# Linear attention into a top-2 mixture of experts: token weights gathered with the row of x, a PSUM bank of its own for the last list products, ScalarE without the list loads

## The chip, the core and the metric

The kernel runs on one core of one Trainium2 chip. Its engines work in parallel, each through its own queue in order: TensorE (PE: matmuls, with weight loads PEld beside them), VectorE (DVE), ScalarE (ACT), GpSimd (POOL, which also issues the indirect DMAs) and SyncE (SP, which issues the plain DMAs). They meet at semaphores, so an instruction that waits holds up all behind it in its own queue. The metric is the device time of one launch in microseconds (us); lower is better.

## The reference, cut to what matters

Block-wise causal linear attention with a decay per head, then a noisy top-2 mixture of experts over its 3072 output rows.

```
x = attention(q, k, v, lam)          # B=4, H=8, S=768, D=64 -> x: 3072 x 512
noisy = x @ w_gate + log1p(exp(x @ w_noise)) * noise        # 3072 x 8
top2 = the two largest of noisy, weights = softmax of the two
for e in range(8):                   # w1[e]: 512 x 1024, w2[e]: 1024 x 512
    rows = tokens with e among their two
    out[rows] += weight * (relu(x[rows] @ w1[e]) @ w2[e])
```

All of it is float32. The kernel makes each expert product of three matmuls, high part by high part, high by low and low by high.

## The kernel before

**Attention.** `for t in range(NST)` runs 12 steps of two 128-token chunks each. A step's output `xo` is multiplied by the gate's weights (`products`, `logits`) and transposed to rows of tokens by `store_x` (TensorE's transposes L419, ScalarE's copy into `xc` L421, SyncE's store into `x_tok` in DRAM L423). ScalarE also takes the attention's transposes out of PSUM (L305 `kT`, L319 `qT`). The loads of weights and their split into a high part (ScalarE L753) and a low part (VectorE L754) are spread over the steps by the tables `LOADS` and `SPLITS`.

**Routing.** The 24 chunks go in three groups (`GB` = 0, 8, 16, 24). For each, `gate` finds the two experts of a token on VectorE, `weights` their two weights on GpSimd (into `wd`, 128 x chunks x 8), `count` and `route` each token's place in its experts' lists. A Python generator per group hands out its VectorE and GpSimd work in small pieces: `advance(n)` puts about n us of pieces behind what stands in the program at that point, so the order is fixed when the program is built, and each engine keeps to it.

**Lists.** The lists of tokens by expert are made by one-hot matmuls. For each unit of one or two chunks, `keys` writes two one-hot tables on VectorE (L578), `loads` makes two products of the second of them, one on ScalarE (L587, by the token's row `rowf`), one on VectorE (L590, by the chunk's number), and `enlist` multiplies the tables on TensorE (L599) into one bank of PSUM, `pL`. That bank also holds the gate's logits and the counts (L522). VectorE adds the result to `found`; `decode` turns it into integers `recs`, two for each place: the token, and where the weight lies in a table `wtab` in DRAM (four VectorE operations, the last of them L617).

**Experts.** `gather_rows` fetches a tile's 128 rows of x by an indirect DMA on GpSimd (L777), `gather_w` a tile's weights from `wtab` by another (L784). `trans_rows` transposes a tile (TensorE L793) and splits it into `xth` (ScalarE L795) and `xtl` (VectorE L796). `gemm1` (L809, with the evictions L815 on ScalarE and L819 on VectorE) and `gemm2` (L847) follow; experts 1 to 7 add what they make to the rows of `out` (gather L831, VectorE L859, scatter L866). The output is zeroed first by 24 plain DMAs (L879).

**The handover.** Expert 0 is started while the second and third group are still being routed, in parts of 2, 2 and 3 tiles (`PARTS0`): the first needs the lists of the first group, the second those of the second, the third those of the third. So the program after the attention runs: first two tiles transposed, first `gemm1`, between them the list products of the second group (`pv` as tables), second part with the gate of the third group in between, then `lists_done` in the middle of the `gemm2` of tile 2 (after 12 of its 24 matmuls, `MID`): the third group's list products, `recs`, then the gathers of the last three tiles of expert 0, of four tiles of expert 1, and of three tiles' weights. From there experts 1 to 7 run one after the other. A last loop (`For_i`) over overflowing tiles runs no times with this data.

Of the kernel before, what the change touches and what calls it, by code (L numbers as in the profile page):

```python
# [24 lines left out]
I32 = mybir.dt.int32  # L25
# [28 lines left out]
RW = 2  # L54
NTL = E * NT
NV = 2
HOT = 2 * (128 + NTL + NV * NTL)
# [8 lines left out]
SPLITS = {2: (1, 0), 3: (1, 1), 6: (1, 2), 7: (1, 3), 9: (2, 0), 10: (2, 1), 11: (2, 2)}  # L66
MID = 12
# [55 lines left out]
def kernel(  # L123
# [16 lines left out]
    x_tok = dram.tile([NTOK, DM], FT, name="x_tok")  # L140
    wtab = dram.tile([128 * NCH * E, 1], FT, name="wtab")
# [24 lines left out]
    zero = consts.tile([128, DM], FT, name="zero")  # L166
# [54 lines left out]
    for nm in ("kt", "qt", "vt"):  # L221
# [25 lines left out]
    WBASE = (BIG // TS) * E + TS * NCH * E  # L247
    wcol = consts.tile([128, E, NT], FT, name="wcol")
    nc.gpsimd.iota(wcol, pattern=[[1, E], [0, NT]], base=WBASE, channel_multiplier=0,
                   allow_small_or_imprecise_dtypes=True)  # L250
    destf = consts.tile([128, 2, NCH], FT, name="destf")
    recs = consts.tile([128, NTL, RW], I32, name="recs")
# [161 lines left out]
    def store_x(u):  # L414

        for a in range(2):
# [6 lines left out]
            nc.sync.dma_start(x_tok[g * C:(g + 1) * C, :], xc.rearrange("p d i -> p (d i)"))  # L423
# [66 lines left out]
    def weights(b):  # L490
# [92 lines left out]
    def loads(b, c, n, buf):  # L583
# [3 lines left out]
        nc.scalar.activation(mv[:, :, 1, :], hi, AF.Copy, scale=rowf)  # L587
# [6 lines left out]
    def enlist(some, start=True, stop=True):  # L594

        LP = pl[:, :NV * NTL]
        pairs = [(lo[:, k, :], mv[:, k, :]) for b, c, n, buf in some for lo, _, mv in (hot(buf, n),) for k in range(2 * n)]
        for k, (lo, mv) in enumerate(pairs):
            nc.tensor.matmul(LP, lo, mv, start=start and not k, stop=stop and k == len(pairs) - 1)  # L599
        b, c, n, _ = some[-1]  # L600
        RT[b]["listed"] = c + n
        if stop:
            LP = LP.rearrange("p (w j) -> p w j", w=NV)
            if "found" in RT:
                nc.vector.tensor_add(found, found, LP)
            else:
                nc.vector.tensor_copy(found, LP)
            RT["found"] = True

    def decode(s, out, n, base):  # L610

        v = nc.vector
        idf = rp.tile([128, 2, n], FT, name=f"idf{n > 1}")
        v.scalar_tensor_tensor(idf[:, 0], s[:, 0], float(TS), s[:, 1], op0=MULT, op1=ADD)
# [595 lines left out]
```

## Time and profile before

| what | us |
|---|---|
| median of 3 runs (lowest, highest) | 783.83 (781.5, 785.53) |
| the profiled execution | 789.62 |
| its span, first to last instruction | 787.7 |
| TensorE busy in the span | 740.5 (94%) |
| VectorE, ScalarE, GpSimd busy | 348.5, 227.8, 289.4 |

All views are of the one profiled execution; times in them are us from the start of its span. A view in order of time gives an instruction's start, its duration, and in brackets how long its engine had been idle before it and what ended that wait. "issue" means that the engine waited for nothing that the profile shows. Line numbers are those of the kernel before. [...]

### The profile page before, as it was taken

How to read it: one execution, taken by the hardware profiler on the slowest of the kernel's cores; microseconds unless marked ns; L12 is line 12 of the kernel's file. 1: busy time of each engine (PE TensorE's matmuls, PEld its weight loads, DVE VectorE, ACT ScalarE, POOL GpSimd, SP SyncE). 2: the span in 40 equal slices, each digit the busy share in tenths (PEclk: the TensorE clock that was granted, in tenths of full speed). 3: DMA queues.
4: the chain of work that ended last, by engine and by line, in shares of the span. 5: the costliest groups of instructions: out<-in, count | busy, mean ns of one | idle time of the engine just before them, and what ended most of it. 6: DMA issues, size and time to landing. Idle time of an engine off the chain costs nothing.

```text
span 787.7 us, 15593 instructions
## 1 busy us (share of the span) xinstructions
PE 740.5 (94%) x6170; PEld 627.1 (80%) x6170; DVE 348.5 (44%) x823; ACT 227.8 (29%) x395; POOL 289.4 (37%) x438
## 2 busy tenths in 40 slices
PE   6999988869979999999999999999999999999993
PEld 4888867768868888798878877987888898889882
DVE  5555777747414554452335232614343352335210
ACT  0355553541204332142214221413132142214100
POOL 2321333305070475325432743274324425222411
PEclk8899998978989999999999999999999999999997
DMA  7999983254080654444344333424442543321110
GB/s 171 198 270 256 238 217 116 103 208 167 4 248 27 175 154 136 156 121 119 92 151 130 101 108 137 138 75 139 126 134 56 173 157 103 91 95 36 50 53 22
DMA packets 90861, 103.45 MB, mean 131 GB/s; under 512 B 37222, under 2 KB 63462, under 8 KB 90784
## 3 DMA queue, kind: packets, MB, share of 16 engines
q1 hardware_dynamic: 77424, 66.11, 31.3%
q0 software_dynamic: 13360, 36.30, 13.9%
q8 instruction: 50, 0.82, 0.4%
q14 instruction: 27, 0.22, 0.1%
HBM read 77.75 MB, written 25.84 MB: 132 GB/s over the span
## 4 chain that ended last, share of the span: by engine, by line
PE 81%; issue 6%; DVE 3%; ACT 3%; DMA 2%; another core or an unknown queue 2%; POOL 1%; SPq 1%; ACTq 0%; POOLq 0%; DVEq 0%
PE pS L809 33%; PE pKV L847 15%; PE pO L847 14%; PE pS L793 3%; PE pS L344 3%; PE pO L356 2%; PE pKV L356 2%; PE pS L303 2%; PE pS L419 1%; PE pO L852 1%; PE pS L391 1%; PE pS L316 1%; DMA QS<-powd 1%; PE pKV L852 1%
## 5 line engine op out<-in xcount | busy, mean ns | idle before, releaser
L809 PE MATMUL pS<-xth,w1h 128*128 128x512 f32 (+3 forms) x544 | 184.8, 340 | 6.0 <-ACT xth L795 4.1
L809 PE MATMUL pS<-xtl,w1h 128*128 128x512 f32 (+3 forms) x544 | 183.2, 337 | 1.0 <-DVE xtl L796 0.7
L809 PE MATMUL pS<-xth,w1l 128*128 128x512 f32 (+3 forms) x544 | 183.0, 336 | 0.4 <-issue 0.4
L819 DVE SCALAR_TENSOR_TENSOR ht<-pS,ht 128x256 fp32r<-128x256 f32 (+3 forms) x176 | 76.3, 456 | 153.9 <-ACT ht L815 139.3
L847 PE MATMUL pO<-w2h,ht 128*128 128x512 f32 x384 | 126.9, 401 | 0.5 <-ACT ht L815 0.5
L847 PE MATMUL pKV<-w2h,ht 128*128 128x512 f32 x384 | 126.2, 400 | 0.0
L866 POOL DMA_INDIRECT out_dram<-ot,rec x46 | 60.4, 1313 | 172.0 <-DVE ot L859 160.8
L815 ACT ACTIVATE ht<-pS 128x512 fp32r<-128x512 f32 (+3 forms) x136 | 65.1, 483 | 189.5 <-PE pS L809 136.7
L809 PEld LDWEIGHTS pS<-xth,w1h 128*128 128x128 f32 x544 | 105.2, 193 | 16.3 <-ACT xth L795 4.8
L809 PEld LDWEIGHTS pS<-xtl,w1h 128*128 128x128 f32 x544 | 105.1, 193 | 10.0 <-DVE xtl L796 1.2
L809 PEld LDWEIGHTS pS<-xth,w1l 128*128 128x128 f32 x544 | 104.9, 193 | 9.9 <-issue 1.1
L795 ACT ACTIVATE xth<-pS 128x512 fp32r<-128x512 f32 (+2 forms) x53 | 30.0, 572 | 206.9 <-PE pS L793 205.3
L847 PEld LDWEIGHTS pO<-w2h,ht 128*128 128x128 f32 x384 | 72.3, 188 | 18.0 <-ACT ht L815 1.0
L847 PEld LDWEIGHTS pKV<-w2h,ht 128*128 128x128 f32 x384 | 72.3, 188 | 16.8
L847 PE MATMUL pKV<-w2l,ht 128*128 128x512 f32 x192 | 76.1, 396 | 0.0
L847 PE MATMUL pO<-w2l,ht 128*128 128x512 f32 x192 | 76.1, 396 | 0.0
L777 POOL DMA_INDIRECT xg<-x_tok,rec x46 | 48.9, 1062 | 14.3 <-issue 12.4
L831 POOL DMA_INDIRECT pv<-out_dram,rec x46 | 47.1, 1023 | 16.9 <-issue 13.6
L784 POOL DMA_INDIRECT wr<-wtab,rec x46 | 45.9, 997 | 16.0 <-issue 15.1
L859 DVE SCALAR_TENSOR_TENSOR ot<-pKV,wr,pv 128x512 f32<-128x512 f32 x21 | 15.8, 751 | 79.9 <-PE pKV L847 79.9
L859 DVE SCALAR_TENSOR_TENSOR ot<-pO,wr,pv 128x512 f32<-128x512 f32 x21 | 15.8, 751 | 79.7 <-PE pO L847 79.7
L332 POOL TENSOR_TENSOR kd<-kt,Mk 128x512 f32<-128x512 f32 x24 | 24.8, 1057 | 64.2 <-PE pR L391 27.5
(220 smaller groups left out, 1011.5 us busy)
## 6 DMA issues: line engine op xcount, KB each, us to landing
wst<-in_moe_w_dram SPq DMA_DIRECT2D x48, 512.0 KB
wst<-in_moe_w_dram SPq DMA_DIRECT2D x32, 256.0 KB
kt<-in_k_dram SPq DMA_DIRECT2D x12, 512.0 KB
qt<-in_q_dram SPq DMA_DIRECT2D x24, 256.0 KB
vt<-in_v_dram SPq DMA_DIRECT2D x12, 512.0 KB
x_tok<-xc SPq DMA_DIRECT2D x24, 256.0 KB
out_dram<-zero SPq DMA_DIRECT2D x24, 256.0 KB
xg<-x_tok,rec POOLq DMA_INDIRECT x46
```

Source lines behind the costliest of these rows:

```text
L332: nc.gpsimd.tensor_mul(kd[:, :, s], kt[:, :, s], mask(s, slice(0, HP), slice(C - 1, C)).to_broadcast([128, HP, 2, D]))
L356: nc.tensor.matmul(PO[u][a][half(g), hp, :], lhs, rhs, start=n == 1, stop=n == (12 if u % NW or a else 8))
L777: nc.gpsimd.indirect_dma_start(out=XG[t][:size(e, t)], out_offset=None, in_=x_tok[:rows, :], in_offset=bass.IndirectOffsetOnAxis(ap=REC[e, ...
L784: nc.gpsimd.indirect_dma_start(out=WR[e % 3][:n, t:t + 1], out_offset=None, in_=wtab, in_offset=bass.IndirectOffsetOnAxis(ap=REC[e, t][:, ...
L795: nc.scalar.activation(hi, p, AF.Copy)
L809: nc.tensor.matmul(p, W1[a][d][:, fs], xt(b, cs)[:, d], start=(d == 0 and i == 0), stop=(d == DB - 1 and i == 2))
L815: nc.scalar.activation(ht(e, 0, f, cs), p, AF.Relu)
L819: nc.vector.scalar_tensor_tensor(ht(e, 1, f, c), p[:, r], 0.0, ht(e, 0, f, c).bitcast(FT), op0=OP.max, op1=SUB)
L831: nc.gpsimd.indirect_dma_start(out=PV[t][:size(e, t), :], out_offset=None, in_=out, in_offset=bass.IndirectOffsetOnAxis(ap=REC[e, t][:, 0: ...
L847: nc.tensor.matmul(p, ht(e, a, f, cs), W2[b][f // 2][:, f % 2, :], start=(i == 0), stop=(i == len(terms) - 1))
L859: nc.vector.scalar_tensor_tensor(o, p, w, pv, op0=MULT, op1=ADD)
L866: st = nc.gpsimd.indirect_dma_start(out=out, out_offset=bass.IndirectOffsetOnAxis(ap=REC[e, t][:, 0:1], axis=0), in_=o, in_offset=None, bo ...
```

## The change

It has four parts.

1. The rows of `x_tok` grow from 512 to 520 numbers (`XW`). The last eight are the token's weights by expert (0 for experts that are not among its two). `wtab`, its index in `recs` and `gather_w` are gone; `store_w` writes a group's `wd` from SyncE into the last eight columns of its rows, in pieces of 32 bytes. A gathered row then brings its weights with it, and `trans_rows` picks the expert's column: for expert 0 by a copy, for the others by comparing `rank` with the place in the order of experts (VectorE, one small operation per tile, and one reduction per expert ahead of `gemm2`). `decode` makes two operations in place of four.
2. The product of `loads` that ScalarE made (L587) is made by VectorE.
3. The list products after the attention have a PSUM bank of their own (`pR`). Those within the attention's steps keep `pL`.
4. Some steps stand elsewhere: the split of the third piece of w2 (`split_w(2, 0, 2)`) moves out of the last attention step to behind the first two tiles' transposes, which themselves move ahead of the second group's remaining routing work; `lists_done` stands ahead of the `gemm2` of tile 2 and no longer within it.

```diff
+XW = DM + E
-    x_tok = dram.tile([NTOK, DM], FT, name="x_tok")
-    wtab = dram.tile([128 * NCH * E, 1], FT, name="wtab")
+    x_tok = dram.tile([NTOK, XW], FT, name="x_tok")
...
-        nc.gpsimd.dma_start(wtab.rearrange("(p c) o -> p (c o)", p=128)[:, GB[b] * E:GB[b + 1] * E],
-                            wd[:, 0].rearrange("p c e -> p (c e)"))
+        r["w"] = wd[:, 0]
+
+    def store_w(b):
+        rows = x_tok[GB[b] * C:GB[b + 1] * C, :].rearrange("(c p) w -> p c w", p=128)
+        nc.sync.dma_start(rows[:, :, DM:XW], RT[b].pop("w"))
...
-        nc.scalar.activation(mv[:, :, 1, :], hi, AF.Copy, scale=rowf)
+        nc.vector.tensor_scalar(mv[:, :, 1, :], hi, rowf, None, op0=MULT)
...
-        LP = pl[:, :NV * NTL]
+        LP = psum.tile([128, NV * NTL], FT, name="pR") if last else pl[:, :NV * NTL]
...
-    def gather_w(e, t):
...
+    def trans_rows(e, t):
...
         nc.vector.tensor_tensor(lo, p, hi.bitcast(FT), op=SUB)
+        if e > 0:
+            nc.vector.scalar_tensor_tensor(W8[e % 2][:n, t, :], rank[:n, 1:], float(e - 1), XG[t][:n, DM + 1:],
+                                           op0=OP.is_equal, op1=MULT)
+        elif not e:
+            nc.vector.tensor_copy(WR[0][:n, t:t + 1], XG[t][:n, DM:DM + 1])
...
     finish(1)
+    for j in range(2):
+        trans_rows(0, j)
+    products(NST - 1)
     advance(50)
-    for j in range(2):
-        trans_rows(j, TS)
-    products(NST - 1)
+    split_w(2, 0, 2)
     head = [mm1(0, 0, PARTS0[0], 0)]
     logits(NST - 1)
     store_x(NST - 1)
+    store_w(1)
...
                 zero_out(3)
                 advance(FILL1)
+                if "w" in RT[2]:
+                    store_w(2)
...
             finish(2)
             advance(50)
-            assert not jobs
+            assert not jobs and "w" not in RT[2]
+            lists_done()
         for t in range(t0, t0 + n):
-            gemm2(0, t, MIDS.get(t))
+            gemm2(0, t)
...
+        nc.vector.tensor_reduce(WR[e % 2], W8[e % 2], axis=AX.X, op=ADD)
```

ScalarE's queue at the handover, before: `xo` is the last attention step's output, `hb` a table of list products, `xth` the first two tiles of expert 0, `xp` the gate's products, `xc` rows for `x_tok`, `ht` the first eviction of `gemm1`.

```order
L378 ACTIVATE xo<-pO 128x512
L378 ACTIVATE xo<-pKV 128x512
L753 ACTIVATE w2h_356<-wst 128x1024
L587 ACTIVATE hb_369<-hb_369,rowf 128x4x56
L795 ACTIVATE xth_362<-pS 128x4x128 x2
L412 ACTIVATE xp<-pR 128x256
L421 ACTIVATE xc<-pS 128x512 x2
L815 ACTIVATE ht<-pS 128x256 x2
```

The same place after the change (tile and line numbers are those of the changed kernel):

```order
L372 ACTIVATE xo<-pO 128x512
L372 ACTIVATE xo<-pKV 128x512
L782 ACTIVATE xth_359<-pS 128x4x128 x2
L406 ACTIVATE xp<-pR 128x256
L747 ACTIVATE w2h_353<-wst 128x1024
L415 ACTIVATE xc<-pS 128x512 x2
L807 ACTIVATE ht<-pS 128x256 x2
```

`xth` and `xp` now stand directly behind `xo`; the split `w2h` stands behind them, and the load of `hb` is no longer in the queue.

TensorE's queue before, at the third group's lists, where `enlist` begins in the middle of a `gemm2` (the pair of rows for L599 comes 16 times):

```order
L847 MATMUL pO<-w2h_355,ht 128x512
L847 MATMUL pO<-w2l_359,ht 128x512
L847 MATMUL pO<-w2h_355,ht 128x512 x2
L847 MATMUL pO<-w2l_359,ht 128x512
L847 MATMUL pO<-w2h_355,ht 128x512
L599 LDWEIGHTS wst
L599 MATMUL pL<-wst 128x112
```

After the change the same products stand behind the last `gemm1` matmul of expert 0's second part (L801):

```order
L801 MATMUL pS<-xth_359,w1h_346 128x256
L801 MATMUL pS<-xtl_360,w1h_346 128x256
L801 MATMUL pS<-xth_359,w1l_350 128x256
L596 LDWEIGHTS wst
L596 MATMUL pR<-wst 128x112
```

They have moved ahead of the whole of that `gemm2` (L837 in the changed kernel), 12 matmuls earlier, and write to the bank `pR`.

SyncE's queue from the last rows of x to the load of the experts' order, after the change; before it was `x_tok<-xc` x4, `out_dram<-zero` x24 and the load:

```order
L417 DMA x_tok<-xc 128x512 x4
L513 DMA x_tok<-wd 128x8x8
L869 DMA out_dram<-zero 128x512 x3
L513 DMA x_tok<-wd 128x8x8
L869 DMA out_dram<-zero 128x512 x21
L725 TENSOR_LOAD order
```

The two stores of weights are new here; 21 of the 24 zero stores stand behind the second of them, which needs the third group's `wd` from GpSimd.

## Rows read from the trace of the kernel before

**Rows 1.** The busy times of the whole span, first part of the page: engine, busy us, share of the span, instructions.

```profile
PE 740.5 (94%) x6170; PEld 627.1 (80%) x6170; DVE 348.5 (44%) x823; ACT 227.8 (29%) x395; POOL 289.4 (37%) x438
```

**Rows 2.** Busy time by stretch (window in us from the span's start: its length; then for PE, PE's weight loads, VectorE, ScalarE and GpSimd the busy us and instructions; the granted TensorE clock as a share of full; the busy share of the DMA engines; GB/s).

```profile
100.00:124.00 24.00, 20.77 (x492) 17.39 (x488) 17.59 (x59) 12.25 (x25) 6.89 (x9) 1.00 0.79 209
...
124.00:133.00 9.00, 6.78 (x102) 4.86 (x94) 7.04 (x20) 1.35 (x3) 6.19 (x6) 0.73 0.22 60
...
160.00:165.00 5.00, 4.89 (x23) 4.89 (x24) 0.06 (x1) 0.53 (x1) 0.00 (x0) 0.50 0.00 0
...
177.49:184.00 6.51, 6.51 (x36) 6.38 (x37) 4.33 (x22) 1.89 (x5) 3.08 (x3) 0.60 1.02 360
...
228.60:234.00 5.40, 5.39 (x19) 5.23 (x20) 0.41 (x1) 0.00 (x0) 3.93 (x7) 0.50 0.75 237
...
265.50:707.00 441.50, 440.97 (x2237) 370.08 (x2237) 174.99 (x293) 119.21 (x189) 189.98 (x248) 1.00 0.41 124
```

**Rows 3.** TensorE in order of time, first two list groups: start us, us, instruction, in brackets the idle time before it and who ended it.

```profile
104.84 1.47 PE L344 MATMUL pS<-qT,kT 64*64 64x128 f32 x30 [0.92 <-ACT xc L421]
...
110.41 0.66 PE L316 MATMUL pS<-identf,qt 128*128 128x128 f32 x4 [1.04 <-ACT kT L305]
...
118.14 1.47 PE L344 MATMUL pS<-qT,kT 64*64 64x128 f32 x30 [1.17 <-ACT xc L421]
```

**Rows 4.** ScalarE in order of time in the same stretch, and one line of VectorE grouped by operation (duration ns min/median/max, first and last start).

```profile
102.85 0.48 ACT L587 ACTIVATE hb<-hb,rowf 128x224 bf16<-128x224 bf16 x1 [3.67 <-DVE hb L578]
...
109.39 0.48 ACT L587 ACTIVATE hb<-hb,rowf 128x224 bf16<-128x224 bf16 x1 [2.90 <-DVE hb L578]
...
L590 DVE TENSOR_SCALAR hb<-hb x12: 183/192/318, 102.8 to 157.9; 128x112 bf16<-128x112 bf16 x12
```

**Rows 5.** The handover from attention to the experts, in order of time, TensorE, ScalarE, VectorE; last the same eight transposes of `store_x` at the handover and once before it.

```profile
159.28 0.58 PE L809 MATMUL pS<-xth,w1h 128*128 128x256 f32 x1 [3.35 <-ACT xth L795]
...
155.12 1.06 ACT L753 ACTIVATE w2h<-wst 128x1024 fp32r<-128x1024 f32 x1
...
157.77 0.48 ACT L587 ACTIVATE hb<-hb,rowf 128x224 bf16<-128x224 bf16 x1 [1.59 <-DVE hb L578]
...
158.16 1.06 ACT L795 ACTIVATE xth<-pS 128x512 fp32r<-128x512 f32 x2
...
158.77 1.29 DVE L796 TENSOR_TENSOR xtl<-pS,xth 128x512 fp32r<-128x512 f32 x2 [0.71 <-ACT xth L795]
...
163.34 1.95 PE L419 MATMUL pS<-identf,xo 128*128 128x128 f32 x8
...
114.28 1.09 PE L419 MATMUL pS<-identf,xo 128*128 128x128 f32 x8
```

**Rows 6.** The list products of the second group, in order of time: TensorE's wait, VectorE ahead of it, then TensorE's wait for the third group's gate and VectorE in that gate.

```profile
177.49 0.93 PE L599 MATMUL pL<-pv 128*128 128x112 bf16 x8 [4.51 <-DVE l L445]
...
170.75 0.69 DVE L754 TENSOR_TENSOR w2l<-wst,w2h 128x512 fp32r<-128x512 f32 x1 [0.75 <-DMA out_dram<-zero]
...
172.69 0.42 DVE L819 SCALAR_TENSOR_TENSOR ht<-pS,ht 128x256 fp32r<-128x256 f32 x1 [0.50 <-ACT ht L815]
...
175.15 0.42 DVE L819 SCALAR_TENSOR_TENSOR ht<-pS,ht 128x256 fp32r<-128x256 f32 x1 [0.50 <-ACT ht L815]
...
176.12 0.19 DVE L590 TENSOR_SCALAR pv<-pv 128x112 bf16<-128x112 bf16 x1
...
189.70 0.19 PE L522 MATMUL pL<-ob,lstrict 128*128 128x64 bf16 x1 [0.77 <-DVE ob L486]
...
181.56 0.42 DVE L819 SCALAR_TENSOR_TENSOR ht<-pS,ht 128x256 fp32r<-128x256 f32 x1 [1.12 <-ACT ht L815]
```

**Rows 7.** The third group's lists: two pieces of the chain of work that ended last (start us, us, what), then VectorE, GpSimd and TensorE in order of time.

```profile
210.06 2.81 PE pO L847 x12
...
212.86 0.80 PE pL L599 x16
...
214.60 0.21 DVE L617 SCALAR_TENSOR_TENSOR recs<-found,idfTrue 128x52 int32<-128x52 f32 x1
...
215.30 1.09 POOL L777 DMA_INDIRECT xg<-x_tok,recs  x1 [18.34 <-DVE recs L617]
...
223.34 0.66 PE L793 MATMUL pS<-identf,xg 128*128 128x128 f32 x4 [0.74 <-issue]
...
226.68 0.46 PE L793 MATMUL pS<-identf,xg 64*128 64x64 f32 x4 [2.67 <-issue]
...
228.60 0.64 PE L809 MATMUL pS<-xth,w1h 128*128 128x320 f32 x1 [1.47 <-issue]
```

**Rows 8.** What bears on the stores of the weights: GpSimd's last step of the third group's weights; SyncE's issues of the 24 zero stores; the stretch in which the 3072 pieces of 32 bytes of `nz` are loaded (columns as in rows 2).

```profile
195.68 0.32 POOL L514 TENSOR_TENSOR wd<-wd 128x64 f32<-128x64 f32 x1
...
166.32 16.29 SPq L879 DMA_DIRECT2D out_dram<-zero  x24
...
57.00:60.50 3.50, 3.50 (x84) 2.75 (x76) 2.17 (x10) 1.97 (x4) 1.99 (x2) 1.00 0.83 137
```

**Rows 9.** The end of TensorE's slow stretch after 124 us, and the start of the next burst of gathers on GpSimd.

```profile
129.93 0.37 PE L356 MATMUL pKV<-at,vt 64*64 64x128 f32 x1 [0.74 <-issue]
...
180.14 1.09 POOL L777 DMA_INDIRECT xg<-x_tok,recs  x1 [24.81 <-DVE gacc L115]
```

**Rows 10.** GpSimd from 265 us to the end, grouped by line: count, busy us, mean ns, idle before it and who ended that.

```profile
L784 POOL DMA_INDIRECT wr<-wtab,rec x46 | 45.9, 997 | 16.0 <-issue 15.1 <-ACT ht L815 0.9
```

More of the change, by code (lines that the diff above doesn't have):

```diff
@@ L164, in load @@
                           sub(src, at, [[2 * D, 128], [S * D, H], [1, 2 * D]]))
-    zero = consts.tile([128, DM], FT, name="zero")
+    zero = consts.tile([128, XW], FT, name="zero")
     nc.vector.memset(zero, 0.0)
@@ L246 @@
                    allow_small_or_imprecise_dtypes=True)
[L247 to L250, printed above, removed]
     destf = consts.tile([128, 2, NCH], FT, name="destf")
-    recs = consts.tile([128, NTL, RW], I32, name="recs")
+    recs = consts.tile([128, NTL], I32, name="recs")
     sel = consts.tile([128, 2 * E], FT, name="sel")
@@ L592, with enlist, decode @@
     found = consts.tile([128, NV, NTL], FT, name="found")
[L594 to L596 removed]
+    def enlist(some, last=True):
+        LP = psum.tile([128, NV * NTL], FT, name="pR") if last else pl[:, :NV * NTL]
         pairs = [(lo[:, k, :], mv[:, k, :]) for b, c, n, buf in some for lo, _, mv in (hot(buf, n),) for k in range(2 * n)]
         for k, (lo, mv) in enumerate(pairs):
[L599 removed]
+            nc.tensor.matmul(LP, lo, mv, start=not k, stop=(k == len(pairs) - 1))
         b, c, n, _ = some[-1]
         RT[b]["listed"] = c + n
[L602 to L610, printed above, removed]
[L612 to L617 removed]
+        LP = LP.rearrange("p (w j) -> p w j", w=NV)
+        if "found" in RT:
+            nc.vector.tensor_add(found, found, LP)
+        else:
+            nc.vector.tensor_copy(found, LP)
+        RT["found"] = True
+    def decode(s, out, n):
+        v = nc.vector
+        idf = rp.tile([128, n], FT, name=f"idf{n > 1}")
+        v.scalar_tensor_tensor(idf, s[:, 0], float(TS), s[:, 1], op0=MULT, op1=ADD)
+        v.tensor_scalar(out, idf, float(BIG + TS), None, op0=ADD)
     def read_lists(a, b):
[L621 removed]
+        decode(found[:, :, a:b], recs[:, a:b], b - a)
     spacer = consts.tile([1, 1], FT, name="spacer")
@@ L672, in xt @@
         return XT[part][i][:, :, c.start - i * TX * TS:c.stop - i * TX * TS]
-    XG = [wp.tile([128, DM], FT, name=f"xg{t}") for t in range(PARTS0[0])]
+    XG = [wp.tile([128, XW], FT, name=f"xg{t}") for t in range(PARTS0[0])]
     for x in XG:
@@ L679 @@
     HB = [ac.tile([128, 2 * HOT], BF, name=f"hb{i}") for i in range(4)]
-    WR = [rp.tile([128, NT], FT, name=f"wr{i}") for i in range(3)]
-    for x in WR:
+    WR = [rp.tile([128, NT], FT, name=f"wr{i}") for i in range(2)]
+    W8 = [rp.tile([128, NT, E - 1], FT, name=f"w8{i}") for i in range(2)]
+    for x in W8:
         nc.gpsimd.memset(x, 0.0)
@@ L766, in load_rec @@
     def load_rec(e, queue=nc.sync):
-        r = recs[:, :NT, :]
+        r = recs[:, :NT]
         if e:
-            r = rp.tile([128, NT, RW], I32, name="rec", bufs=3)
-            queue.dma_start(r.rearrange("p (e t) w -> p e t w", e=1),
-                            recs.rearrange("p (e t) w -> p e t w", e=E)[:, EXP[e], :, :])
+            r = rp.tile([128, NT], I32, name="rec", bufs=3)
+            queue.dma_start(r.rearrange("p (e t) -> p e t", e=1), recs.rearrange("p (e t) -> p e t", e=E)[:, EXP[e], :])
         for t in range(tiles(e)):
-            REC[e, t] = r[:size(e, t), t, :]
+            REC[e, t] = r[:size(e, t), t:t + 1]
     def gather_rows(e, t, rows=NTOK):
@@ L978, in lists_done @@
             gather_rows(1, j)
-        for j in range(4, 7):
-            gather_w(0, j)
-    MIDS = {2: lists_done}
     for i, (t0, n) in enumerate(parts(0)):
@@ L1009 @@
                 for j in X1[f - 4]:
-                    trans_rows(j, size(1, j))
+                    trans_rows(1, j)
         if i == 2:
```

69 lines of the change are left out of this document (28 added, 41 removed).

## Prediction

> **What bounds the kernel now.** I read the busy times first [rows 1]: TensorE works 740.5 of 787.7 us, so 47 us is the most that any removal of waits can give, the faster clock aside. The table by stretches [rows 2] tells where they lie: from 265.5 to 707 us TensorE is busy 440.97 of 441.5 us at the full clock. What the change does there on VectorE and GpSimd can give nothing; it can only cost. All that can be won lies before 234 us, at four places, which I then read in order of time: two rounds of list building under attention [rows 3, 4], the handover [rows 5], the second group's lists [rows 6], the third group's [rows 7]. Each has two prices: the wait itself, and the clock after it. From 100 to 124 us the waits of 0.92, 1.04 and 1.17 us left the granted clock at 1.00 [rows 2, 3]; after 3.35 us of idling the stretch from 160 to 165 us ran at 0.50, the lower level, and so did the one from 228.6 to 234 us behind waits of 0.74, 2.67 and 1.47 us [rows 2, 5, 7]. The same eight transposes take 1.95 us there and 1.09 us at full clock [rows 5]: 44% less.
>
> The sum is made on the profiled execution (789.62 us, 5.8 above the median of 783.83); I take the saving off the median.
>
> **A. ScalarE makes no loads (100 to 124 us).** Each load held ScalarE 0.48 us, and, being in its queue, it also made ScalarE wait for VectorE's keys: 3.67 and 2.90 us [rows 4]. What is queued behind are the evictions `xc` and `kT`, and for them TensorE waited 0.92 + 1.04 + 1.17 = 3.1 us [rows 3]: the upper bound. The four loads go to VectorE. There the product of half their size takes 192 ns (median; 318 at most) [rows 4], so a load costs 0.2 to 0.4 us, say 0.3, and four 1.2. If all of that came back on TensorE, 1.9 is left: the lower bound. VectorE is busy 17.59 of 24 us in this stretch [rows 2], so about half of it should be hidden: **2.5**.
>
> **B. The handover (155 to 168 us).** ScalarE's queue ran `w2h` (1.06 us from 155.12), waited 1.59 us for VectorE's keys, made the load (0.48), and only at 158.16 began `xth`, for which TensorE had waited 3.35 us [rows 5]. Now `xth` stands directly behind `xo` and can begin near 155.3: 2.86 us earlier. VectorE's `xtl` follows it (1.29 us for two); between its two halves stands one new copy of a column, which I put at 0.14 us, close to the shortest VectorE operation shown, 0.19 [rows 6]. That leaves **2.7**. At worst VectorE, with the last units' two loads still ahead of `xtl` (2 x 0.3) and both copies (2 x 0.14), is 0.9 later: 1.8. If TensorE idles about half a us here, like the waits in A, it keeps the clock: from 160 to 165 us it was busy 4.89 us at 0.50 [rows 2], and 44% of that is **2.1** (0 if the clock falls all the same, 2.4 at exactly half). The split of `w2h` loses nothing behind `xp`: the piece after it is split only at 170.75 [rows 6], in time for the same `gemm2`, and VectorE's half now stands behind `xtl`.
>
> **C. The second group's lists (170 to 190 us).** TensorE waited 4.51 us for its list products. The row names VectorE's logits operation, because those products shared the bank `pL` with the gate; that operation is long done, and the last to come is the last unit's table (176.12 + 0.19, with ScalarE's load beside it) [rows 6]. The bank of its own takes the false order away; what stays is VectorE. There, four small loads come in (4 x 0.2 = 0.8) and three waits go that arose behind ScalarE's loads (0.75, 0.50, 0.50; the first row names a DMA, but ScalarE's half of the same split had been late). 176.31 + 0.8 - 1.75 = 175.4 against a start at 177.49: **2.1**, and a wait of some 2.4 us stays. If those three waits stay too, 0.4. Two fewer operations in `decode`, at 0.21 [rows 7], are **0.3** of `recs`. In the gate of the third group, VectorE waited 1.12 us for ScalarE's `ht` with TensorE waiting for `ob` at its end [rows 6]; if `ht` comes sooner, half of it, **0.6** (0 to 1.1). I count nothing for the clock: the stretch from 177.49 to 184 us ran at 0.60, and a wait of 2.4 us is nearer to those that ended in the lower clock.
>
> **D. The third group's lists (210 to 234 us).** The products move ahead of twelve matmuls of `gemm2`, 2.81 us in the chain of waits, which stood between the tables (long ready) and `recs` [rows 7]. With two operations less in `decode` (0.4) the gathers start 3.2 us sooner. Behind them TensorE waited 0.74 and 2.67 us, 3.4 together, for rows to land, named "issue"; the 1.47 us behind is the last tile's own split and stays [rows 7]. Rows of 2080 in place of 2048 bytes take off perhaps 0.3 (0 to 1.3, should they also meet the last zero stores): **2.9**. With those waits gone, the clock should hold from 228.6 to 234 us, where TensorE was busy 5.39 us at 0.50 [rows 2]: 44%, **2.4**. The three gathers of weights here go too (from 224.49 on GpSimd), but they stood behind the gathers of x and cost nothing.
>
> On the longer rows the rows here only give a landing time: from 215.30 to 226.68 us, 11.4 us for the last one waited for [rows 7]. [...]
>
> **E. The slow stretch after 124 us.** TensorE is busy 6.78 of 9 us there at 0.73, with four gathers on GpSimd, two of them of weights [rows 2, 9]. It is the first burst; the one at 180.14 [rows 9] has no such effect. I take 0; up to 5 if the two gathers are its cause.
>
> **F. Experts 1 to 7.** 46 gathers of weights leave GpSimd (997 ns each, 45.9 us in all [rows 10]); 46 small operations and seven reductions come to VectorE, which is busy 174.99 of 441.5 us [rows 2]. The cover is TensorE's own queue: **0**. A reduction stands ahead of the first `gemm2` of an expert and delays VectorE's evictions by less than one of them.
>
> **G. The stores of weights.** SyncE writes 1024 pieces of 32 bytes for each group. 3072 such pieces were loaded within the stretch from 57 to 60.5 us, at a DMA share of 0.83 [rows 8], so about 1 us a store. The first group's weights are made beside its first tables (102.85 [rows 4]) and gathered after 124 us; the second's store stands where the zero stores began, 166.32 [rows 8], 14 us ahead of its gathers at 180.14 [rows 9]. The third waits for GpSimd's `wd` (195.68 + 0.32 [rows 8]); behind it in SyncE's queue stand 21 zero stores, which took 16.29 us for 24 [rows 8], so 14.3. 196 + 1 + 14.3 = 211.3, and the next gathers start at 215.30 - 3.2 = 212.1: **0**, with under 1 us to spare.
>
> **Sum.** A 2.5, B 2.7 + 2.1, C 2.1 + 0.3 + 0.6, D 2.9 + 2.4, E to G 0: 15.6. 783.8 - 15.6 = **768** (774 for an execution like the profiled one). All lower bounds: 1.9 + 1.8 + 0.7 + 1.9 = 6.3, so 777.5. All upper ones without E: 3.1 + 5.1 + 3.5 + 5.9 = 17.6, so 766; with 2.3 for the clock in C and 5 for E, 759.
>
> **The rivals.**
> - **The clock stays low** at the handover and in D though the waits shrink: 4.5 us back, 772.5. For it: three of the places have it now, and some waits stay. Against it: waits of about 1 us under attention left it at 1.00. Chance 0.20.
> - **VectorE becomes the late one.** All that ScalarE made now stands in VectorE's queue ahead of the same tables and evictions, so most waits are renamed, not removed: the lower bounds, 777.5. For it: from 124 us VectorE is busy 7.04 of 9 us [rows 2], and in C a wait for its last table stays in any case. Against it: in A it has 6 us free. Chance 0.13.
> - **The slow stretch goes too**, because half of its gathers do: 763. Chance 0.10.
> - **Slower: the third store.** If its 1024 pieces take t us and not 1, the 21 zero stores, and the load of the experts' order behind them, move into the gathers that TensorE waits for in D. From t = 2 on each us is a us in D; from t = 17.5 on it eats the whole 15.6, at 21.5 the kernel is 0.5% slower, at 25 it is 791. For it: each piece is a write of 32 bytes, and no row here shows such writes. Against it: the loads of `nz`. Chance 0.05. [...]
> - **No change**: the waits come back further on, since experts 1 to 7 are held by something other than TensorE. 440.97 of 441.5 us speak against it. Chance 0.03.
>
> **How the numbers follow.** The forecast has 0.49, the rivals the rest. What a measurement can tell is about 0.5%, 3.9 us: faster means under 779.9. Forecast, low clock, slow stretch and most of the VectorE case are there: 0.88. Same: 0.07 (a part of the VectorE case, no change, a mild third store). Slower: 0.05. The range holds the low clock and the lower bounds, up to 778.5, and the slow stretch below, down to 760.
>
> **What would show it.** A: no wait on `xc` or `kT` over 0.5 us from 100 to 124 us. B: TensorE's wait ahead of the first `gemm1` near 0.5 us and a granted clock near 1.00 behind it. C: a wait of 2 to 3 us ahead of the list products, ended by the last table on VectorE. D: the first of the three gathers some 3 us nearer to the end of `gemm1`, waits ahead of the transposes of 0.5 us together, full clock behind. F: experts 1 to 7 in the same 441 us. It is wrong if the zero stores still run once the third gathers have begun, if TensorE waits for VectorE's tables longer than now, or if experts 1 to 7 take over 1 us longer.

## The result, and the profile after

The changed kernel takes 758.23 us (median of 4 runs, 756.73 to 759.9) against 783.64 before: a ratio of 0.9677 (95% interval 0.9645 to 0.9709), 25.4 us less. The forecast was 768 with a range down to 760. On other chips the kernel before took 790 to 792 us and the changed one 757 to 760, so the ratio there is 0.960 to 0.961. Times of experiments are therefore compared on one chip; where the stages of traces from two chips are compared, the text says so.

The page of the changed kernel, first the span, then busy times; they answer to [rows 1]: TensorE's 740.5 us became 728.7 with the same 6170 matmuls; the granted clock, taken over the span, rose from 0.969 to 0.986.

```profile
span 756.3 us, 15517 instructions
...
PE 728.7 (96%) x6170; PEld 619.4 (82%) x6170; DVE 353.1 (47%) x891; ACT 222.4 (29%) x381; POOL 234.8 (31%) x380
```

The stretches that answer to [rows 2] (columns as there): lists under attention; the slow stretch; from the first `gemm1` to the second group's lists; these lists and the third gate; what follows; behind the third gathers.

```profile
100.00:124.00 24.00, 23.40 (x612) 20.87 (x608) 22.17 (x69) 13.18 (x25) 9.73 (x11) 1.00 0.77 224
124.00:133.00 9.00, 7.32 (x115) 6.33 (x115) 8.21 (x34) 2.91 (x5) 2.40 (x11) 0.81 0.17 57
...
146.70:157.70 11.00, 10.48 (x88) 10.26 (x88) 6.11 (x19) 6.36 (x14) 0.00 (x0) 1.00 0.38 124
157.70:170.60 12.90, 9.47 (x58) 7.95 (x57) 11.87 (x71) 2.20 (x5) 3.51 (x9) 1.00 0.15 42
170.60:176.60 6.00, 5.97 (x33) 4.86 (x33) 4.58 (x20) 0.00 (x0) 4.42 (x19) 0.72 0.00 0
207.00:218.00 11.00, 10.81 (x72) 10.58 (x73) 3.37 (x14) 2.19 (x5) 7.33 (x12) 1.00 0.72 230
```

The clock stays at 1.00 at the handover and behind the third gathers, where it was 0.50. From 157.7 to 170.6 us VectorE is busy 11.87 of 12.9: it is the bound there now, and TensorE idles 3.4 us. Behind that the clock is 0.72 in the mean of six us: it is 0.50 for 3.4 of them and 1.00 for the rest. In the traces of both kernels the clock has these two values alone; a figure between them is a mean.

TensorE's waits at the places of [rows 5 to 7], in order of time: the first `gemm1`, the second group's lists (two waits in place of one), the third gate's counts, the last of the third group's tiles, the `gemm1` behind them.

```profile
146.72 0.38 PE L801 MATMUL pS<-xth,w1h 128*128 128x256 f32 x1 [0.34 <-ACT xth L782]
...
158.97 0.26 PE L596 MATMUL pR<-pv 128*128 128x112 bf16 x2 [0.86 <-DVE pv L587]
...
160.20 0.26 PE L596 MATMUL pR<-pv 128*128 128x112 bf16 x2 [0.97 <-DVE pv L587]
...
170.63 0.19 PE L519 MATMUL pL<-ob,lstrict 128*128 128x64 bf16 x1 [1.62 <-DVE ob L480]
...
206.09 0.46 PE L780 MATMUL pS<-identf,xg 64*128 64x64 f32 x4 [0.51 <-DMA xg<-x_tok,recs]
...
207.02 0.41 PE L801 MATMUL pS<-xth,w1h 128*128 128x320 f32 x1 [0.47 <-ACT xth L782]
```

3.35 us became 0.34; 4.51 became 0.86 and 0.97; 0.74 and 2.67 became 0.51. The wait for the third gate grew, from 0.77 to 1.62.

Cutting each trace at the same events (the first `store_x` transposes of attention's steps 5 and 9, the first `gemm1`, the end of the second group's list products, the first transposes of expert 0's tiles 2 and 3, expert 1's first transposes, the start of the last scatter) gives the us of each stretch. Two traces stand for each kernel, since the profiled execution before the change was a long one; `before_again` and `after_again` are the same kernels once more, on two different chips. Single stretches of one kernel differ by up to 5 us from trace to trace, so a difference of two traces in one row is a rough figure.

| stretch | before | before_again | after | after_again | second less fourth | forecast |
|---|---|---|---|---|---|---|
| start to step 5 | 90.7 | 93.3 | 88.1 | 89.5 | 3.9 | 0 |
| steps 6 to 9 (A, E) | 52.9 | 50.8 | 45.8 | 44.3 | 6.5 | 2.5 |
| to the first gemm1 (B) | 15.6 | 15.7 | 12.9 | 12.7 | 2.9 | 2.7 |
| to the second lists (B's clock, C) | 19.1 | 18.4 | 13.7 | 13.8 | 4.6 | 4.2 |
| to tiles 2 and 3 (C) | 17.4 | 17.0 | 17.8 | 16.8 | 0.1 | 0.9 |
| to expert 1 (D) | 48.0 | 43.4 | 39.9 | 40.1 | 3.3 | 5.3 |
| experts 1 to 7 (F) | 531.6 | 530.3 | 530.1 | 530.2 | 0.1 | 0 |
| last scatter to the end | 12.4 | 12.5 | 8.0 | 7.9 | 4.5 | 0 |
| sum | 787.7 | 781.3 | 756.3 | 755.3 | 26.0 | 15.6 |

The stretches for which something was forecast gave 17.4 us against 15.6, but that nearness is in part luck: steps 6 to 9 gave 4.0 us more than forecast, the stretch to expert 1 2.0 less. The rest, 8.4 us, lies at the two ends of the span, where the prediction read nothing.

### The profile page after: what moved, and what is told of

Read it like the earlier page. It is cut to its first block, busy times and chain, and to the rows that moved or that the text cites. A ratio compares the mean times of both kernels' runs of the same rounds, so it can differ in the third digit from the quotient of the medians.

```text
span 756.3 us, 15517 instructions
## 1 busy us (share of the span) xinstructions
PE 728.7 (96%) x6170; PEld 619.4 (82%) x6170; DVE 353.1 (47%) x891; ACT 222.4 (29%) x381; POOL 234.8 (31%) x380
## 5 line engine op out<-in xcount | busy, mean ns | idle before, releaser
L801 PE MATMUL pS<-xth,w1h 128*128 128x512 f32 (+3 forms) x544 | 181.7, 334 | 1.6 <-ACT xth L782 1.6
L801 PE MATMUL pS<-xtl,w1h 128*128 128x512 f32 (+3 forms) x544 | 180.5, 332 | 1.2 <-DVE wr L788 1.2
L801 PE MATMUL pS<-xth,w1l 128*128 128x512 f32 (+3 forms) x544 | 180.5, 332 | 0.0
L837 PE MATMUL pKV<-w2h,ht 128*128 128x512 f32 x384 | 127.5, 403 | 0.0
L837 PE MATMUL pO<-w2h,ht 128*128 128x512 f32 x384 | 126.4, 400 | 0.0
L801 PEld LDWEIGHTS pS<-xth,w1h 128*128 128x128 f32 x544 | 102.5, 188 | 11.1 <-ACT xth L782 2.4
L801 PEld LDWEIGHTS pS<-xtl,w1h 128*128 128x128 f32 x544 | 102.8, 189 | 10.4 <-DVE wr L788 1.8
L801 PEld LDWEIGHTS pS<-xth,w1l 128*128 128x128 f32 x544 | 102.4, 188 | 8.9
L837 PEld LDWEIGHTS pKV<-w2h,ht 128*128 128x128 f32 x384 | 73.1, 190 | 17.0
L837 PEld LDWEIGHTS pO<-w2h,ht 128*128 128x128 f32 x384 | 72.3, 188 | 16.8
L837 PE MATMUL pKV<-w2l,ht 128*128 128x512 f32 x192 | 76.6, 399 | 0.0
L837 PE MATMUL pO<-w2l,ht 128*128 128x512 f32 x192 | 76.1, 396 | 0.0
L748 DVE TENSOR_TENSOR w2l<-wst,w2h 128x1024 fp32r<-128x1024 f32 (+1 forms) x33 | 39.3, 1191 | 11.6 <-ACT w2h L747 11.6
```

What stands on the lines that cost most here:

```text
L748: nc.vector.tensor_tensor(lo[:, r], st[:, r], hi[:, r].bitcast(FT), op=SUB)
L801: nc.tensor.matmul(p, W1[a][d][:, fs], xt(b, cs)[:, d], start=(d == 0 and i == 0), stop=(d == DB - 1 and i == 2))
L837: nc.tensor.matmul(p, ht(e, a, f, cs), W2[b][f // 2][:, f % 2, :], start=(i == 0), stop=(i == len(terms) - 1))
```

## The experiments

**One part alone, and the kernel before once more** (one chip; before 784.38 us). `only_rows` is before with part 1, `only_loads` with part 2, `only_order` with part 4.

> The kernel before, unchanged, for a second trace. Theory G (the two gathers of weights): TensorE's slow stretch in the attention step after the first gathers returns at the same place, 4 to 6 us long, and the first step's output again leaves PSUM near 28 us. Rival H (chance of one execution): the stretch is gone or stands elsewhere, the first step's output comes 2 us earlier or later, and the 12 us between the last scatter's start and the end of the span shrink to about 8.

> The kernel before with part 1 alone (weights behind the rows of x, gather_w gone). Theory G: the slow stretch after the first gathers loses its cause, 4 to 5 us, and two operations less in decode give some 0.4 us at the third lists: 778 to 780 us. Rival H: only the 0.4 us, 783 us. Rival (third store): the zero stores run into the gathers, over 786 us.

```diff
-        nc.gpsimd.dma_start(wtab...[:, GB[b] * E:GB[b + 1] * E], wd[:, 0]...)
...
+        nc.sync.dma_start(rows[:, :, DM:XW], RT[b].pop("w"))
...
-                gather_w(0, j)
```

> The kernel before with part 2 alone (VectorE makes both products of loads). Theory A: TensorE's three waits of 3.1 us on xc and kT go, 2.5 us of it stay gained, the handover loses the 0.5 us load and the wait before it (2 us), the second list products come 1 us sooner: 778 to 779 us. Rival (VectorE the late one): 782 us or more, with TensorE's wait ahead of the second list products over 4.5 us.

```diff
-        nc.scalar.activation(mv[:, :, 1, :], hi, AF.Copy, scale=rowf)
+        nc.vector.tensor_scalar(mv[:, :, 1, :], hi, rowf, None, op0=MULT)
```

> The kernel before with part 4 alone (the split behind the first transposes, lists_done ahead of gemm2). Theory: the first gemm1 begins 2.7 us sooner at full clock (2 to 2.7 more), the third gathers 2.8 us sooner with the clock behind them held (4 us with it, the waits of 0.74 and 2.67 us gone): 772 to 775 us. Rival (the clock stays low at both places): 778 us.

```diff
+    for j in range(2):
+        trans_rows(j, TS)
+    products(NST - 1)
     advance(50)
-    for j in range(2):
-        trans_rows(j, TS)
-    products(NST - 1)
+    split_w(2, 0, 2)
...
+            lists_done()
```

Measured: `before_again` 783.09 us; its steps 6 to 9 took 50.8 us and not 52.9, the end again 12.5 us. The slow stretch of [rows 9] was not there, but the next step lost 3 us to another wait (below): H for the form, G for the loss. `only_rows` 777.57 (ratio 0.9902, 0.9868 to 0.9935), `only_loads` 778.06 (0.9909, 0.9882 to 0.9937), `only_order` 779.09 (0.992, 0.9889 to 0.9952). The loads came out as expected. The order gained 5 us and not 10, the number of the rival that the clock stays low, but not for its reason: the first 5 us behind the first `gemm1` and behind the third gathers ran at 1.00. The stretch to expert 1, where the order was to gain most, took 43.4 us in this trace of before and not 48.0, and 40.4 in `only_order`; the rows gained what G said, but 4.3 us of it at the end of the span (8.1 us from the last scatter), which no theory had; its steps 6 to 9 took 50.2 us, only 0.6 less than in `before_again`.

**One part undone** (another chip; before 792.14 us; the changed kernel with an unused table, `dummy_table` below, took 759.48 there and serves as its measure). `no_rows`, `no_loads` and `no_order` are the changed kernel with the three diffs above reversed; `no_bank` has its own.

> The changed kernel with part 1 undone (wtab and gather_w back; parts 2 to 4 stay). Additive theory: the parts act at their own places, so it loses what part 1 alone gained, 6.8 us: 765 us, of which 4.3 us lie between the start of the last scatter and the end of the span (12.4 us again and not 8.1). Rival (coupling): the attention phase also falls back to the 127 us from the first to the last step's output that the single parts have (119 with all of them), 770 us or more.

> The changed kernel with part 2 undone (ScalarE makes one product of loads again). Additive theory: 758.2 + 6.3 = 764.5 us. Rival (coupling): the handover's order and the bank give their full gain only without ScalarE's loads, so 768 us or more, with TensorE's wait ahead of the second list products back above 3 us.

> The changed kernel with part 3 undone (all list products in pL). Theory as predicted in C: the false order behind the gate's logits returns and TensorE waits some 2 us longer ahead of the second list products: 760 to 761 us. Rival (the bank was only named, the last table was late in any case): 758 to 759 us.

```diff
-        LP = psum.tile([128, NV * NTL], FT, name="pR") if last else pl[:, :NV * NTL]
+        LP = pl[:, :NV * NTL]
```

> The changed kernel with part 4 undone (split, transposes and lists_done where they stood). Additive theory: 758.2 + 5.3 = 763.5 us. Rival (coupling, the clock): the waits at the handover and in front of expert 0's last three tiles return and take the clock with them, 10 us or more: 768 us or more.

Measured: `no_rows` 778.44 us, `no_loads` 765.85, `no_bank` 760.1, `no_order` 767.41. The order is worth 7.9 us, the loads 6.4, the bank 0.6, which four runs each do not tell from nothing (the stretch to the second lists took 14.7 us for 13.8), and the rows 19, far more than alone. The loads fit the additive theory (6.3), the order lies between its two (5.3 and 10), and the rows gave what the rival of coupling said in its total. The rows also move tiles, which is taken up below, so the 19 us are not the gathers alone. Of `no_rows` against `dummy_table`, 5.6 us lie in steps 6 to 9, 6.0 behind the third lists, 1.9 in the experts, 4.7 at the end. Behind the third lists TensorE of `no_rows` waited for ScalarE's copies `xth`; GpSimd, then TensorE, in order of time:

```profile
210.93 0.99 POOL L784 DMA_INDIRECT wr<-wtab,recs  x1 [0.30 <-issue]
212.23 0.99 POOL L784 DMA_INDIRECT wr<-wtab,recs  x1 [0.30 <-issue]
213.53 0.95 POOL L784 DMA_INDIRECT wr<-wtab,recs  x1 [0.31 <-issue]
```

```profile
219.48 0.64 PE L809 MATMUL pS<-xth,w1h 128*128 128x320 f32 x1 [5.76 <-ACT xth L795]
```

The `gemm1` begins 5.76 us after TensorE's last transpose, where the changed kernel's waits 0.47; in `dummy_gathers`, below, it waits 3.98, in `powd_first` 6.81. In no row is it seen what holds ScalarE. It happens behind the three gathers of single numbers, but not each time: `before_again`, `only_loads`, `only_order` and `before_pad` have the same gathers and wait 0.47.

**The gathers themselves, the stores, the first group's gathers** (a third chip; before 791.51 us).

> The changed kernel, unchanged, for a second trace beside the next three. Expected: the same gain, 24 to 27 us against before on this chip; the two attention steps behind the first gathers 23.7 to 25.4 us together (25.4 to 29.4 with the weights' gathers or ScalarE's loads), 8.0 us from the last scatter's start to the end. If the 2.6 us by which its first trace was ahead at 88 us were luck, this trace begins later.

> The changed kernel with 53 gathers of single numbers put back on GpSimd at the places where gather_w stood, from a table of zeros that nobody uses; all else stays. Theory G (the gathers themselves cost): the attention steps behind the first gathers take 2.5 to 3.5 us more, the end 4.4 us more (12.4 us again), the third gathers up to 2: 7 to 10 us slower than the changed kernel. Rival H (what cost was the plain stores to wtab, the index and luck): within 1 us of the changed kernel, end at 8.0 us.

```diff
+                gather_w(0, j)      # at all four places; reads a table of zeros into a tile nobody uses
```

> The changed kernel with its three stores of weights issued by GpSimd (as before) and not by SyncE. Theory G: the end stays at 8.0 us, and the time within 1 us. Rival for the end (plain DMAs on GpSimd's queue, not the number of gathers, made it long): 12.4 us there, 4.4 us slower.

```diff
-        nc.sync.dma_start(rows[:, :, DM:XW], RT[b].pop("w"))
+        nc.gpsimd.dma_start(rows[:, :, DM:XW], RT[b].pop("w"))
```

> The kernel before, with only the first group's two gathers of weights moved from the attention step to behind the last rows of x. Theory G: GpSimd's next products kd come 2.6 us sooner, and the two attention steps behind the first gathers take 26 us together and not 27.4 to 29.4; 1.5 to 3 us faster than before, the end still 12.4 us. Rival H: same as before within 1 us, those steps 27.4 us or more.

```diff
                 gather_rows(0, j, GB[1] * C)
-                gather_w(0, j)
...
     store_x(NST - 1)
+    for j in range(PARTS0[0]):
+        gather_w(0, j)
```

Measured: `after_again` 759.85 us (0.9613, 0.957 to 0.9656), `dummy_gathers` 769.55 (0.9751, 0.9688 to 0.9813), `plain_store` 761.73 (0.9639), `late_w0` 787.58 (0.994, 0.9913 to 0.9966). G holds at its three places, with more than it said at the third (5.6 us for up to 2): with the gathers back steps 6 to 9 took 49.1 us, the stretch to expert 1 45.7 (45.1 and 40.1 in `after_pad` below, on another chip, whose attention tiles lie alike), the end 12.7. Its total of 9.7 us is in part luck, since the tiles that the dummies write moved others, which cost at the beginning and gained in the experts (below). With the first two gathers moved away from attention, before gained 3.9 us; the trace of `late_w0` is that of its longest run and tells little of the place. `plain_store` fits neither side: its end is 9.8 us.

A part of what attention suffers is seen on VectorE and GpSimd. In order of time, VectorE and then GpSimd of the changed kernel:

```profile
119.54 2.60 DVE L97 SCALAR_TENSOR_TENSOR gacc<-gacc,gu 128x64 f32<-128x64 f32 x3
...
122.66 2.04 DVE L455 SCALAR_TENSOR_TENSOR gn<-gn,ge 128x64 f32<-128x64 f32 x8
```

```profile
116.87 1.27 POOL L770 DMA_INDIRECT xg<-x_tok,recs  x1 [8.09 <-DVE recs L611]
118.44 1.00 POOL L770 DMA_INDIRECT xg<-x_tok,recs  x1 [0.30 <-issue]
119.47 2.06 POOL L326 TENSOR_TENSOR kd<-kt,Mk 128x512 f32<-128x512 f32 x2
```

The same operations in `before_again`, VectorE, GpSimd, and TensorE's wait that came of it:

```profile
129.19 0.73 DVE L98 SCALAR_TENSOR_TENSOR gacc<-gacc,gu 128x64 f32<-128x64 f32 x3
...
130.44 4.66 DVE L461 SCALAR_TENSOR_TENSOR gn<-gn,ge 128x64 f32<-128x64 f32 x8
```

```profile
130.63 1.00 POOL L784 DMA_INDIRECT wr<-wtab,recs  x1 [0.30 <-issue]
131.66 2.06 POOL L332 TENSOR_TENSOR kd<-kt,Mk 128x512 f32<-128x512 f32 x2
```

```profile
136.74 1.66 PE L303 MATMUL pS<-identf,kt 128*128 128x128 f32 x8 [3.23 <-DVE at L347]
```

While GpSimd makes `kd` (2.06 us), VectorE's gate hardly moves: three operations take 2.60 us where they take 0.73 beside gathers, eight take 4.66 where they take 2.04. By what means `kd` slows it is not shown. Attention's `kd` stands behind the gathers in GpSimd's queue: it starts 2.60 us after the first of them here (116.87 to 119.47) and 5.07 us in the profiled run of before (124.14 to 129.21). It holds up VectorE's `at`, for which TensorE waits, in both kernels; later it meets other operations and costs 2.6 us and not 1.9. That wait was 3.23 us in the three kernels of the first chip that have four gathers (`before_again`, `only_loads`, `only_order`), 2.55 in `only_rows`, which has two. So the difference that goes with two gathers is 0.7 us here. In the other traces the loss takes the form of [rows 9], gaps of TensorE that nothing shown ended: from 112 to 140 us six or seven of at least 0.25 us, 1.7 to 2.2 us together, in before, `before_pad`, `no_rows` and `dummy_gathers` (four, 1.08 us, in `powd_first`), against one to three, 0.55 to 0.84 us, in the eleven kernels there with two gathers or with the first two moved. So the form goes with the chip or the execution, and the size with the number of gathers.

**The two ends of the span** (the second chip; before 791.83 us).

> The changed kernel with the table wtab allocated again in DRAM and zeroed by one plain DMA in the fourth step, and no gathers. Open: why the first store of attention's constants (powd) is read back at 6.9 to 7.1 us in all kernels without gather_w and at 7.6 to 7.9 us in all with it, with 2.3 us more by the first transposes of an output. Theory T (the table's place or zeroing in DRAM): 7.6 to 7.9 us here and about 2 us slower than the changed kernel. Theory N (the number of GpSimd's indirect DMAs in the program): 6.9 to 7.1 us, within 1 us of the changed kernel. End 8.0 us in both.

```diff
+    wtab = dram.tile([128 * NCH * E, 1], FT, name="wtab")      # and zeroed at t == 3
```

> The changed kernel with 28 gathers of single numbers from such a table put back in experts 1 to 4 alone, 180 indirect DMAs in all. Theory for the end: GpSimd's last drain (3.18 us with 152 of them, 7.43 to 7.67 with 205 to 208) grows with their number, 5 to 6 us here, an end of 10 us; rival (it is one or the other by a threshold): 3.2 or 7.4. Theory G for the experts: TensorE's time in them is unchanged, and the attention steps behind the first gathers take 23.7 to 25.4 us as without dummies.

```diff
+                        if e <= 4:
+                            gather_w(e, f)
```

> The kernel before with powd allocated in DRAM ahead of x_tok and wtab. Theory T (the place in DRAM): powd is read back at 6.9 to 7.1 us and the first transposes come 2 us sooner, 2 us faster than before. Theory N: 7.6 to 7.9 us and no change.

```diff
+    powd = dram.tile([H, 2, 256], FT, name="powd")
     x_tok = dram.tile([NTOK, DM], FT, name="x_tok")
```

Measured: 759.48, 759.04 and 791.9 us (ratios 0.9578, 0.958, 0.9991). The end: GpSimd's last DRAIN stands between TensorE's last matmul and the end of the span. From the traces' instructions that no view counts as busy:

```
kernel         indirect DMAs  last DRAIN (us)  last scatter to the end (us)
after               152            3.18               8.0
dummy_half          180            5.39              10.1
dummy_gathers       205            7.43              12.7
before              205 + 3 plain  7.67              12.4
plain_store         152 + 3 plain  4.98               9.8
```

28 and 53 more gathers cost 2.2 and 4.25 us, 80 ns for each one added. Those between 152 and 205 add up evenly, so the rival's jump is not there; the 152 that all kernels have cost far less than 80 ns each (3.18 us in all, at most 21 ns each), so the line does not go down to none. The three plain stores of `plain_store`, of 1024 pieces each, cost 1.8; those of before, to `wtab`, come with 0.24 (7.67 for 7.43). For the beginning T fell: powd was read back at 7.08 us in `dummy_table`, which T put at 7.6 or more, and at 7.78 in `powd_first`, which it put at 7.1 or less. N fits these two and `dummy_half` (7.85); it falls with `after_pad` below, which has 152 indirect DMAs and reads at 7.85. And the experts ran 4.8 us faster in the two kernels with dummy gathers (`dummy_gathers`, `dummy_half`) than in any other: 460.8 us from expert 1's first to the last scatter, 465.6 to 466.8 in the others so far.

**The places of the tiles** (a fourth chip; before 790.14 us). What these odd ones share is where the tiles start in SBUF.

> The changed kernel with one unused tile of 32 bytes a partition in SBUF, ahead of the pool that holds ht. In the two kernels with dummy gathers in the experts, expert 1's first to the last scatter took 460.82 us, in all others 465.66 or more. What those two had in common is the place of ht: a multiple of 64 bytes, as w2 is in the changed kernel (before: ht a multiple, w2 32 bytes off; changed: w2 a multiple, ht 32 off). Theory P (place): 460.8 us here, 4.8 us faster than the changed kernel. Rival: 465.7 us, the small gathers themselves did it.

```diff
+    rp.tile([128, 8], FT, name="pad")
     N1 = E - 1
```

> The kernel before with two unused tiles of 32 bytes, so that w1, w2 and ht all stand at multiples of 64 bytes. Theory P: 460.8 us from expert 1's first to the last scatter and 4 to 5 us faster than before. Rival: 465.7 us or more and no change.

```diff
+    consts.tile([128, 8], FT, name="pad")
...
+    rp.tile([128, 8], FT, name="pad1")
```

> The changed kernel, unchanged, as the measure beside after_pad on the same chip: 756 to 760 us, 465.7 us from expert 1's first to the last scatter.

Measured: `after_pad` 762.77 us (0.9657, 0.9635 to 0.968), `before_pad` 787.3 (0.998, 0.9957 to 1.0003), `after_third` 757.03 (0.9595, 0.9566 to 0.9625). The experts took 464.2 us in `after_pad` and 464.4 in `before_pad`: 1.4 us of the 4.8, so a multiple of 64 bytes, as P has it, is not what the dummies had. The traces and the compiled programs tell more. Nearly all of the 4.8 us lies in `gemm2`, whose matmuls read w2 and `ht`: from the start of one to the start of the next they take 247.0 us in the changed kernel, 245.5 in the two pads, 242.3 in the two dummies. And the distance in SBUF from w2 to `ht`, less whole multiples of 128 bytes, is 0 in the two pads, 64 in the two dummies and 96 in the other sixteen, which take 246.9 to 248.0. That fits all 20 traces, but no run moved `ht` alone.

But the 32 bytes made the whole kernel 5.7 us slower (the runs of the two kernels do not overlap). They moved all that is allocated behind them, attention's tiles too. In the compiled programs `kt`, `qt`, `vt`, `xc` and `xo` start at a multiple of 64 bytes in the changed kernel and in all others that read powd back at 6.85 to 7.14 us, and 32 bytes off in all that read it at 7.61 to 7.89: before, `after_pad` and the two kernels with dummy gathers among them, 20 traces without an exception. SyncE in order of time, the store of powd and its read, of the changed kernel and of `after_pad`:

```profile
4.87 0.30 SPq L199 DMA_DIRECT2D powd<-xc  x1
6.97 1.37 SPq L202 DMA_DIRECT2D at<-powd  x2
```

```profile
4.87 0.30 SPq L199 DMA_DIRECT2D powd<-xc  x1
7.85 1.36 SPq L202 DMA_DIRECT2D at<-powd  x2
```

`after_pad` needed 93.1 us to step 5, `after_third` 87.0. That pair overstates it: the nine traces with attention's tiles at a multiple of 64 needed 87.0 to 93.3 us to step 5, 90.1 in the mean, the eleven others 90.7 to 95.2, 92.6 in the mean. Of the 2.5 us between the means 2.2 are there by the first step's `store_x` (35.1 against 37.3 us). Four traces (`only_rows`, `no_bank`, `dummy_table`, `only_loads`) spend 15 to 16 us on step 3 where the others spend 10 to 12, for a reason not looked for; without them the means are 88.9 and 92.4. That the place of these tiles costs the time, rather than what goes with it, is argued from this agreement. Part 1's tiles (recs of half the size, wider `XG`, `W8`) had shifted attention's by chance.

## Why the prediction was wrong

- **Direction and most steps held.** B's wait: 2.9 us for 2.7, with a wait of 0.34 left, and the clock at 1.00 behind it. B's clock and C's lists: 4.6 for 4.2; but the bank is worth at most 0.9 of it (`no_bank`), not 2.1: in `only_loads`, which has no bank of its own, the wait ahead of the lists was already 2.42 us for 4.75. What brings the lists forward is the queue without ScalarE's loads and the clock. C's gain on the gate did not come (0.1 for 0.9): VectorE, with the loads of both kinds, is the bound there (busy 11.87 of 12.9 us), as the second rival said, at this one place.
- **F is the step that failed.** "The cover is TensorE's own queue" holds within experts 1 to 7 (530.3 us in `before_again`, 530.1 in the changed kernel) and not for what comes after TensorE's last matmul. There GpSimd drains, which took 7.67 us before and 3.18 after, and the end of the span shrank by 4.4 us: 80 ns for each of the 53 gathers, as `dummy_gathers` and `dummy_half` show. No row for it was read, nor any of the span's last 12 us; the signs of being wrong looked at the middle too. That the sum of all upper terms, 759, came near 758.2 is luck: it had 5 us for E and nothing for the two ends.
- **E was the rival taken for nothing.** "I take 0" was wrong: two gathers less were worth 0.6 us in steps 6 to 9 on the first chip (`only_rows`) and some 4 us elsewhere (`late_w0` 3.9 in all, `dummy_gathers` 4.0 against `after_pad`, from two chips). Of that `kd` and VectorE's gate explain 0.7 us. The burst at 180.14, which was held against it, has no `kd` behind it.
- **A was mis-sized.** The loads alone gained 2.0 and 1.7 us in its two steps (`only_loads`: step 7 took 11.0 us for 13.0, step 8 10.5 for 12.2), 3.7 in place of 2.5. The three waits shown, 3.1 us, were taken for the upper bound; but step 8 gained 1.7 with a shown wait of 1.16, at a clock of 1.00 in both. The idle time in brackets was not all that the stall had cost there.
- **D's gathers of weights did not "cost nothing" each time.** The products ahead of `gemm2` came 2.8 us sooner, as forecast: 0.12 us behind the last `gemm1` matmul in place of 2.93. But the three gathers behind them went with 5.6 us in `dummy_gathers` against `after_pad` (two chips) and 6.0 in `no_rows` against `dummy_table`, though with no late copy in four other traces. D as a whole gave 8.1 us against the profiled execution, 3.3 against `before_again`. Nor is the clock behind the third gathers always held: in `after_third` it was 0.66 from 203 to 208 us.
- **No step named the places of tiles.** Widening rows and halving `recs` moved every tile allocated after them. `after_pad` shows what 32 bytes are worth in the changed kernel: 5.7 us. That the step from before to the changed kernel gained as much from it was not shown by itself; of the 3.9 us in the first stretch, 2.5 to 3.5 is the difference of the means of the two groups of traces.
- **The wider rows** cost little, if anything: from the third group's first gather to the last tile's transposes the twelve traces with rows of 2080 bytes took 10.6 to 12.5 us (11.3 in the mean), the eight with 2048 bytes 10.1 to 11.6 (11.1). The 0.3 us that D's sum takes off for them was the author's estimate: no run shows that term by itself, and the two means differ by 0.2 us. The third store took no time: 21 zero stores were issued from 177.4 to 191.4 us, before the gathers at 195.0. The trace names a zero store ahead of the first of these, but it starts 0.83 us behind `recs`, as in `plain_store` (0.85), where all zero stores were issued by 169.0.

## What stays open

How gathers of single numbers on GpSimd make TensorE's gaps and ScalarE's late copies, and why the first chip shows neither (nor `before_pad`, on the fourth, the late copies), was not found: that the gaps go with these gathers is shown by `dummy_gathers`, `no_rows` and `late_w0`, and for the late copies by the first two; by what means is not. Why the rows are worth 19 us beside the other parts and 6.8 alone is explained in part only. That the distance from w2 to `ht` sets `gemm2`'s pace is read from 20 traces and was not tried: a version with attention's tiles as in the changed kernel and `ht` moved alone, to where the dummies had it, would show it, and could gain up to 4.8 us more.

## What to carry to other kernels

Read the first and the last us of a span as closely as the middle: work that is hidden behind the bounding engine may still be paid for at the end, when its own engine drains: here 80 ns for each gather added. An edit that changes the size of a tile moves all that are allocated behind it, and 32 bytes can be worth more than an edit (5.7 us in `after_pad`, where the bank was worth 0.6); print the tiles' addresses of both versions before the gain is put down to the edit. The idle time shown ahead of a stalled instruction need not be all that the stall costs: step 8 of `only_loads` gained 1.7 us where 1.16 were shown. And compare groups of traces, not one pair, before a difference of a few us in one stretch is put down to the edit.

## What the runs showed that was not expected

GpSimd's last drain grew by 80 ns for each indirect DMA added to the program (3.18 us at 152, 5.39 at 180, 7.43 at 205). VectorE's small operations lost 1.9 to 2.6 us beside GpSimd products of 2.06 us. A store from tiles 32 bytes off a multiple of 64 was read back at 7.61 to 7.89 us for 6.85 to 7.14, in 20 traces. `gemm2`'s matmuls in the experts took 247.0, 245.5 or 242.3 us, by where w2 and `ht` lay. On a chip where the kernel before took 8 us more (791.51 for 783.64), the changed one took the same to 2 us (759.85 for 758.23).
